# Linear attention and a top-1 mixture of experts on one core: routing arrays and k's maximum moved into PSUM, logits scaled on GpSimd, weight halves on VectorE, and the queues in another order

## The chip, the cores and the metric

The kernel runs on one NeuronCore of one Trainium2 chip. The metric is the device time of one execution in microseconds (us). Its five engines are written as in the profile: PE (TensorE, with PEld for its weight loads), DVE (VectorE), ACT (ScalarE), POOL (GpSimd) and SP (SyncE, which here only issues transfers). Each engine takes its instructions strictly in the order in which the program lists them, so an instruction that waits holds up everything behind it on its engine.

## What is computed

Inputs are `q`, `k`, `v` of shape 8 x 8 x 576 x 64 (batch, heads, sequence, head size), a gate matrix of 512 x 8, and two weight matrices for each of eight experts. The reference, cut to what matters:

```python
q_s = exp(q - max(q, axis=-1));  q_s /= sum(q_s, axis=-1)      # softmax over the 64 of a head
k_s = exp(k - max(k, axis=2));   k_s /= sum(k_s, axis=2)       # softmax over the 576 of the sequence
x   = einsum('bhsd,bhde->bhse', q_s, einsum('bhsd,bhse->bhde', k_s, v))   # then 4608 tokens x 512
logits = x @ w_gate                                            # 4608 x 8
expert = argmax(logits);  gate = softmax(logits)[expert]
out = gate * (relu(x @ w1[expert]) @ w2[expert])
```

## The kernel before, in words

The program has three stages.

*Attention.* The eight batches are taken one by one. For each batch SP loads k, v and q. DVE takes k's maximum (`k_max`, lines 135 to 141, step `ka`) over the nine rows that a partition holds: a chain of four instructions that halve nine rows to one. PE turns the result (`kt`, line 147), DVE reduces it across what were partitions (`kr`, line 154), PE spreads it back (`kx`, line 161), ACT copies it to SBUF (`ky`, line 167). POOL subtracts it from k (`ks`, line 173, three pieces of three rows), ACT takes the exponential (`ke`, line 181), and PE accumulates k times v (`v`, lines 190 and 200) in two PSUM banks. DVE divides by the sums (`vd`, `vr`, `vm`, lines 206 to 213), PE and ACT turn the result and multiply it with the gate matrix (`vt`, `vc`, `vg`, `vh`, lines 219 to 234). For q, DVE takes row maxima (`qm`, line 240), POOL subtracts (`qc`, line 248), PE turns (`qt`, line 256), ACT takes the exponential (`qe`, line 261), PE forms the product (`x`, line 270), which also carries eight gate logits per head, and ACT copies it out of PSUM (`xo`, line 282). The denominators are then prepared and inverted (`xd`, `xr`, lines 286 and 290) and the logits multiplied with them (`xl`, line 296, on DVE).

*Routing.* Two batches make a pair, whose 1152 tokens lie as 9 tiles of 128. Twenty small steps (`route`, lines 315 to 415), each one `r` in the order, sum the logits, find the largest, make a one-hot array, count tokens before each one with matmuls (line 364 on), and compute the row and tile that each token will have among those of its expert. They are almost all on DVE and their arrays, of 9 or 72 numbers a partition, lie in SBUF. `store` writes the pair's tokens to DRAM.

*Experts.* Tokens are gathered in tiles of 128 by expert (`g`, line 519, an indirect transfer that POOL issues), split into high and low 16-bit parts (`ps`, `ph`, `pl`), multiplied with w1 (`f`, line 598), passed through relu (`fh`, `fl`), multiplied with w2 (`s`, line 632), scaled and scattered. The weights are split into high and low parts as well: for the first expert `sh` makes the high part on ACT and, for w1, `ss` scales on ACT (line 677) and `sp` subtracts on POOL (`split_low_pool`, line 682); for w2, `sl` does both in one DVE instruction (`split_low`, line 673). For the other experts `ah` and `aw` do so and write both halves to DRAM, and POOL issues the indirect loads of line 745 that bring them back. From tile 3 on, `run` repeats one fixed order for each tile; I call this the loop. The first expert is chosen before the last pair is routed (`fe`), so that three tiles (slots 0 to 2) can be gathered and multiplied early.

The order of attention and of the passage into the loop is not found by a scheduler when the kernel is built: two tables of steps, `ATTENTION` and `JOIN`, list it, and `emit` (line 975) issues each step's instructions on its engines in that order. `ka:3` is the maximum of batch 3, `ks:3:6:3` its rows 6 to 8, `r:2` the next two routing steps.

PSUM has eight banks. Before, three pools share them: `ps_t` with two one-bank buffers, which serve k's turned maximum, its spread copy, both accumulators of k times v and the routing counts in turn; `ps_q` with two one-bank buffers; and `ps_x` with two buffers of two banks for the products.

Of the kernel before, what the change touches and what calls it, by code (L numbers as in the profile page):

```python
# [59 lines left out]
class Attention:  # L60


    def __init__(self, nc, tc, ctx, kctx, q, k, v, w_gate, xsc, R, C):
# [71 lines left out]
    def k_max(self, L, g=None):  # L135
        V, gs, k, m = self.nc.vector, self.heads(g), L["kt"], self.tile(L, "m", self.k1, [P, HP, D])
        t = self.tile(L, "mw", self.k1, [P, HP, 4, D])
        V.tensor_tensor(t[:, gs], k[:, gs, 0:4, :], k[:, gs, 4:8, :], op=ALU.max)
        V.tensor_tensor(t[:, gs, 0:2], t[:, gs, 0:2], t[:, gs, 2:4], op=ALU.max)
        V.tensor_tensor(t[:, gs, 1], t[:, gs, 1], k[:, gs, 8, :], op=ALU.max)  # L140
        V.tensor_tensor(m[:, gs], t[:, gs, 0], t[:, gs, 1], op=ALU.max)
# [139 lines left out]
    def x_out(self, L, m):  # L281
        self.nc.scalar.copy(self.x_rows(L, m, 1)[:, 0, 0:XU].rearrange("p (a x) -> p a x", a=2), L["xp", m][:, :, 0:4 * KW])  # L282
# [9 lines left out]
    def x_logit(self, L, j, n):  # L292

        u = self.x_units(L, j, n)
        lg = u[:, :, :, D + 1:KW]
        self.nc.vector.tensor_tensor(lg, lg, u[:, :, :, D:D + 1].broadcast_to([P, n, H, NE]), op=ALU.mult)
# [18 lines left out]
    def route(self, L):  # L315
# [85 lines left out]
        def row_int():  # L401
            V.tensor_single_scalar(T["ri"][:, :], T["ri"][:, :], P - 1, op=ALU.bitwise_and)
# [8 lines left out]
        def tile_no():  # L411
            V.tensor_tensor(R["rt"][:, ts], T["rank"][:, :], T["rm"][:, :], op=ALU.subtract)
# [587 lines left out]
lk:0:0 xi:0 xi:1 xi:2 lk:0:1 lk:1 ka:0:0 ka:0:1 lq:0 kt:0 kr:0 kx:0 ky:0 ka:1 lv:0 ks:0:0:3 kt:1 kr:1 qm:0:0:4  # L1000
kx:1 ks:0:3:3 ke:0:0:3 qm:0:4:5 lk:2 ky:1 ks:0:6:3 ke:0:3:3 v:0:0:3 ks:1:0:3 ke:0:6:3 lq:1 v:0:3:3 ks:1:3:3
ke:1:0:3 v:0:6:3 ks:1:6:3 ke:1:3:3 vd:0 lv:1 vr:0 vm:0 qc:0:0:2 vt:0 ke:1:6:3 vc:0 qc:0:6:2 qm:1:0:4 qt:0:0 vg:0
qe:0:0 qc:0:4:2 qm:1:4:5 lk:3 vh:0 x:0:0 qc:0:2:2 qc:0:8:1 xo:0:0 qt:0:1 qc:1:0:2 v:1:0:3 qe:0:1 lq:2 qc:1:6:2
v:1:3:3 qc:1:4:2 v:1:6:3 qc:1:2:2 qc:1:8:1 lv:2 qt:0:2 vd:1 qt:0:3 ka:2 qe:0:2 x:0:1 qe:0:3 x:0:2 xo:0:1 vr:1
# [105 lines left out]
```

## Time and profile before

| what | value |
|---|---|
| median of three runs | 661.26 us (659.49 to 662.1) |
| profiled execution, its own time | 659.28 us |
| its span, first to last instruction | 657.6 us (1.7 us lie around it) |
| mean granted PE clock | 0.943 of full speed |
| PE, DVE, ACT, POOL busy | 84%, 55%, 40%, 51% of the span |
| first product of batch 0, last of batch 7 | start 28.6 us, end 167.8 us |
| first w1 matmul | 180.2 us |
| first w1 matmul of tile 3 (start of the loop) | 217.0 us |

How to read it: the averages over the span hide that the three stages have different limits. The loop and what ends it take 440.6 of the 657.6 us, and their code is the same in both kernels. A window is a stretch of the span, in us from its start; the profile gives busy time by engine for each. A wait is put down to the instruction that released it.

### The profile page before, as it was taken

The page shows a single profiled execution, that of the slowest core. Times are in us where ns is not written, and L with a number is a line of the kernel's source. Part 1 is how long each engine was busy: PE and PEld are TensorE (multiplying, and loading weights), DVE is VectorE, ACT ScalarE, POOL GpSimd, SP SyncE. Part 2 cuts the span into 40 slices and gives each one's busy share as a digit, 9 for nine tenths or more (in the row PEclk, how much of TensorE's full clock was granted, in tenths as well). Part 3 has the DMA queues.
Part 4 walks back from the last instruction along what each step waited for, and adds up shares of the span by engine and source line. Part 5 has one row for each costly group of instructions (what it writes and reads, how often), then busy time and mean ns, then how long its engine had stood idle before and what let it go on. Part 6 is the DMA issues. An engine that isn't in the chain of part 4 may idle for free.

```text
span 657.6 us, 18347 instructions
## 1 busy us (share of the span) xinstructions
...
## 2 busy tenths in 40 slices
...
GB/s 316 325 347 119 335 243 219 167 167 272 239 206 306 271 307 182 217 330 268 221 248 309 287 201 199 153 269 146 247 175 374 219 181 207 203 178 80 149 148 12
DMA packets 73526, 148.58 MB, mean 226 GB/s; under 512 B 32721, under 2 KB 32721, under 8 KB 69843
## 3 DMA queue, kind: packets, MB, share of 16 engines
...
HBM read 220.73 MB, written 50.42 MB: 412 GB/s over the span
## 4 chain that ended last, share of the span: by engine, by line
PE 19%; issue 19%; DMA 15%; POOL 14%; DVE 1%; POOLq 1%; ACT 1%; ACTq 0%
DMA w<-wh,widx 11%; PE ps_q L632 9%; POOL w L745 9%; PE ps_x L598 9%; DMA out_dram<-ysb,sm 4%; POOL xg L519 3%; POOL out_dram L640 2%; PE ps_t L580 1%; DMA wh<-qs 0%; POOLq L745 0%; ACT xn L561 0%; PE ps_t L869 0%; DVE qs L719 0%; DVE co L719 0%; DVE w L673 0%
## 5 line engine op out<-in xcount | busy, mean ns | idle before, releaser
L745 POOL DMA_INDIRECT w<-wh,widx x140 | 144.7, 1034 | 167.7 <-PE ps_q L632 121.3
L598 PEld LDWEIGHTS <-w 128*128 128x128 f16 x3744 | 213.0, 98 | 27.4 <-DMA w<-wh,widx 14.9
L632 PE MATMUL ps_q<-w,ht 128*128 128x512 f16 x936 | 215.2, 386 | 15.2 <-DMA w<-wh,widx 11.7
L598 PE MATMUL ps_x<-xt,w 128*128 128x128 f16 x3696 | 214.7, 220 | 15.7 <-DMA w<-wh,widx 10.3
L632 PEld LDWEIGHTS <-ht 128*128 128x128 f16 x936 | 90.9, 99 | 121.6 <-issue 20.8
L607 DVE SCALAR_TENSOR_TENSOR ht<-ps_x,ht 128x512 f16<-128x512 f32 x77 | 53.0, 691 | 135.1 <-ACT ht L603 135.1
L603 ACT ACTIVATE ht<-ps_x 128x512 f16<-128x512 f32 x77 | 45.6, 596 | 139.4 <-PE ps_x L598 112.6
L173 POOL TENSOR_TENSOR kt<-kt,ms 128x768 f32<-128x768 f32 x24 | 47.9, 2026 | 33.2 <-ACT ms L167 22.7
L640 POOL DMA_INDIRECT out_dram<-ysb,sm x39 | 43.9, 1126 | 39.5 <-ACT ysb L636 23.2
L636 ACT ACTIVATE ysb<-ps_q,sm 128x512 f32<-128x512 f32 x39 | 26.8, 687 | 71.1 <-issue 35.9
L519 POOL DMA_INDIRECT xg<-xsc,gidx x40 | 39.2, 980 | 23.1 <-DVE sl_rank L926 11.4
L561 ACT ACTIVATE xn<-xg,sm 128x512 f16<-128x512 f32 x39 | 28.3, 726 | 52.8 <-DVE sm L556 36.8
L200 PEld LDWEIGHTS ps_t<-vt,kt 64*64 64x64 f32 x1152 | 38.2, 154 | 14.3 <-issue 13.8
L566 DVE SCALAR_TENSOR_TENSOR xn<-xg,sm,xn 128x512 f16<-128x512 f32 x39 | 29.3, 751 | 31.4 <-ACT xn L561 31.3
L200 PE MATMUL ps_t<-vt,kt 64*64 64x128 f32 x1152 | 42.6, 305 | 2.7 <-issue 2.7
L248 POOL TENSOR_TENSOR qs<-qt,qm 128x512 f32<-128x512 f32 x32 | 37.1, 1187 | 9.9 <-PE ps_q L219 7.1
L553 DVE TENSOR_TENSOR xg<-xg 128x512 f32<-128x512 f32 x39 | 27.4, 702 | 10.6 <-DMA xg<-xsc,gidx 7.2
L719 DVE SCALAR_TENSOR_TENSOR qs<-kt,qs 128x1024 f16<-128x1024 f32 x20 | 24.0, 1222 | 12.8 <-ACT qs L712 12.8
L270 PE MATMUL ps_x<-kvb,qT 64*64 64x73 f32 x1152 | 29.2, 251 | 2.1 <-ACT xmain L282 1.1
L261 ACT ACTIVATE qT<-ps_q 128x512 f32<-128x512 f32 x36 | 20.8, 596 | 24.5 <-PE ps_q L256 17.4
L582 ACT COPY xt<-ps_t 128x1024 f16<-128x1024 f16 x29 | 29.2, 1007 | 0.6 <-PE ps_t L580 0.6
L270 PEld LDWEIGHTS ps_x<-kvb,qT 64*64 64x64 f32 x1152 | 24.9, 153 | 6.9 <-issue 4.0
(173 smaller groups left out, 536.2 us busy)
## 6 DMA issues: line engine op xcount, KB each, us to landing
...
```

What stands on the lines that cost most here:

```text
L173: (eng or self.nc.gpsimd).tensor_tensor(kt, kt, m.unsqueeze(2).broadcast_to([P, gs.stop - gs.start, n, D]), op=ALU.subtract)
L200: nc.tensor.matmul(L["kv", h][a * D:(a + 1) * D, c, :], kt[r, g, i, :], v, start=False, stop=(i == NR - 1 and c == 1))
L248: (eng or self.nc.gpsimd).tensor_tensor(qs.rearrange("p i g d -> p g i d"), L["qt"][:, :, j:j + n, :], m, op=ALU.subtract)
L270: self.nc.tensor.matmul(xp[i * D:(i + 1) * D, a, u * KW:(u + 1) * KW], L["qT", m][r, 2 * i + c, h * D:(h + 1) * D], kvb[i][r, c, h, :], st ...
L519: self.nc.gpsimd.indirect_dma_start(out=self.xg[j % self.NX][:, :], out_offset=None, in_=self.xsc[0:rows, :], in_offset=bass.IndirectOffse ...
L566: self.nc.vector.scalar_tensor_tensor(self.heads(xn[:, 1, :]), self.xv(j), self.sm[j % self.NX][:, 2:3], self.heads(xn[:, 0, :]), op0=ALU. ...
L598: self.nc.tensor.matmul(ps[:, s * P:(s + 1) * P], self.w1[c // 2][:, c % 2, lo, f], xt[:, a, :], start=(c == 0 and k == 0 and s == 0), sto ...
L603: self.nc.scalar.activation(self.ht[j % 2][:, hf, 0:4, :].rearrange("p s t -> p (s t)"), ps, AF.Relu)
L607: self.nc.vector.scalar_tensor_tensor(ht[:, hf, 4:8, :].rearrange("p s t -> p (s t)"), ps, 0.0, ht[:, hf, 0:4, :].rearrange("p s t -> p (s ...
L632: self.nc.tensor.matmul(yp[:, :], ht[:, hf, a, :], self.w2[hf][:, s // 2, lo, s % 2, :], start=(c == 0 and k == 0), stop=(c == 7 and k == 2))
L640: self.nc.gpsimd.indirect_dma_start(out=self.out[:, :], out_offset=bass.IndirectOffsetOnAxis(ap=self.sm[j % self.NX].bitcast(I32)[:, 4:5], ...
L745: self.nc.gpsimd.indirect_dma_start(out=t.rearrange(flat), out_offset=None, in_=self.halves[which - 1][h][0:rows].rearrange("r a b f -> r ...
```

## The change

1. **PSUM shared out anew.** The two `ps_x` buffers are no longer handed out in turn. One (`xp`) holds every product, so there is one product buffer instead of two. Of the other, one bank (`room`) holds routing arrays, and one (`mx`) holds k's turned maximum and its spread copy, which leave the `ps_t` pool.
2. **Routing arrays in `room`** for the first three pairs: all arrays but `mx`, `ex` and `km`, the counts among them. The last pair keeps them in SBUF. `tile_no` masks bits and copies where it subtracted.
3. **k's maximum in one instruction**: `k_max` becomes a single reduction over nine rows, read with a step of 64 numbers. (Two new functions, `k_pair` and `k_max_pair`, are in the file, but no step of the tables calls them.)
4. **Logits scaled on POOL** instead of DVE (`x_logit`).
5. **w1's low parts for the first expert on DVE**: the tables use `sl` where they used `ss` and `sp`.
6. **Both tables are new**: the same steps in another order.

The diff, cut to its core (of the tables, a line each of many):

```diff
-        self.idle = self.ps_x.tile([P, 2, 512], F32, name="ps_x")[:, 0, :]
+        self.xp = self.ps_x.tile([P, 2, 512], F32, name="ps_x")
+        both = self.ps_x.tile([P, 2, 512], F32, name="ps_x")
+        self.room, self.mx, self.idle = both[:, 0, :], both[:, 1, :], both[:, 1, 0:256]
...
     def k_max(self, L, g=None):
-        V, gs, k, m = self.nc.vector, self.heads(g), L["kt"], self.tile(L, "m", self.k1, [P, HP, D])
-        t = self.tile(L, "mw", self.k1, [P, HP, 4, D])
-        V.tensor_tensor(t[:, gs], k[:, gs, 0:4, :], k[:, gs, 4:8, :], op=ALU.max)
-        V.tensor_tensor(t[:, gs, 0:2], t[:, gs, 0:2], t[:, gs, 2:4], op=ALU.max)
-        V.tensor_tensor(t[:, gs, 1], t[:, gs, 1], k[:, gs, 8, :], op=ALU.max)
-        V.tensor_tensor(m[:, gs], t[:, gs, 0], t[:, gs, 1], op=ALU.max)
+        gs, m = self.heads(g), self.tile(L, "m", self.k2, [P, HP, D])
+        self.nc.vector.tensor_reduce(m[:, gs], L["kt"][:, gs].rearrange("p g i d -> p g d i"), axis=AX.X, op=ALU.max)
...
-        L["mt", g] = mt = self.ps_t.tile([P, len(gg), 2, D], F32, name="ps_t")
+        L["mt", g] = mt = self.mx[:, 0:len(gg) * P].rearrange("p (a h q) -> p a h q", a=len(gg), h=2)
...
-        L["mb", g] = mb = self.ps_t.tile([P, len(gg) * 2, D], F32, name="ps_t")
+        L["mb", g] = mb = self.mx[:, 256:256 + len(gg) * P].rearrange("p (g d) -> p g d", g=2 * len(gg))
...
-        L["xp", m] = xp = self.ps_x.tile([P, 2, 512], F32, name="ps_x")
+        xp = self.xp
...
-        self.nc.vector.tensor_tensor(lg, lg, u[:, :, :, D:D + 1].broadcast_to([P, n, H, NE]), op=ALU.mult)
+        self.nc.gpsimd.tensor_tensor(lg, lg, u[:, :, :, D:D + 1].broadcast_to([P, n, H, NE]), op=ALU.mult)
...
+        room, used = (self.room if bp + 1 < NBP else None), [0]
...
         def t(name, shape, dt=F32):
-            T[name] = self.p2.tile(shape, dt, name=name)
+            if room is None or name in ("mx", "ex", "km"):
+                T[name] = self.p2.tile(shape, dt, name=name)
+            else:
+                n = shape[1] * (shape[2] if len(shape) > 2 else 1)
+                a = room[:, used[0]:used[0] + n]
+                used[0] += n
+                a = a if dt == F32 else a.bitcast(dt)
+                T[name] = a if len(shape) == 2 else a.rearrange("p (a b) -> p a b", a=shape[1])
...
         def tile_no():
-            V.tensor_tensor(R["rt"][:, ts], T["rank"][:, :], T["rm"][:, :], op=ALU.subtract)
+            V.tensor_single_scalar(T["ri"][:, :], T["ri"][:, :], -P, op=ALU.bitwise_and)
+            V.tensor_copy(R["rt"][:, ts], T["ri"][:, :])
...
-xd:7:4:1 xr:7:2:2 ph:1 xr:7:4:1 al:8 xl:7:2:2 sh:2:0 xl:7:0:2 xl:7:4:1 ps:0 rq:7 sh:2:1 al:11 sh:2:2 r:1 ph:0
+f:1:0 rq:7 ah:8 r:1 al:9 f:1:1 r:3 f:1:2 r:1 sh:2:0 r:5 sl:2:2 r:1 ah:9 sl:2:0 ah:10 f:1:3 ah:11 r:2 f:0:0 r:6
```

The last two lines are the heart of the new `JOIN`: the early tiles' w1 matmuls (`f:1`, `f:0`) now stand ahead of and among the last pair's routing (`rq:7` and the `r` behind it). Before, the first `f` stood behind all of it.

The order of the instructions on an engine, at three places. On DVE, in the middle of attention, around the second half of the first pair's routing, before (`rk` and `cnt` are the counts and their running sum, `ri` and `rm` integer rank and row, `m` k's maximum, `mw` its intermediate):

```order
93 L386 TENSOR_TENSOR rk<-ps_t,cnt 128x72
94 L390 TENSOR_TENSOR rk<-rk,oh 128x72
95 L393 TENSOR_TENSOR cnt<-cnt,ps_t 128x8
96 L396 TENSOR_REDUCE rank<-rk 128x9
97 L399 CAST ri<-rank 128x9
98 L138 TENSOR_TENSOR mw<-kt_168 128x1024
99 L139 TENSOR_TENSOR mw<-mw 128x4x128
100 L140 TENSOR_TENSOR mw<-mw,kt_168 128x4x64
101 L141 TENSOR_TENSOR m<-mw 128x256
102 L402 TENSOR_SCALAR ri<-ri 128x9
103 L405 CAST rm<-ri 128x9
```

The same stretch now, with `ps_x` as the name of the bank `room` (and, in the row of `cm`, of `mx`):

```order
62 L139 TENSOR_REDUCE m<-kt_171 128x256
63 L403 TENSOR_TENSOR ps_x<-ps_x,cnt 128x72
64 L407 TENSOR_TENSOR ps_x<-ps_x,oh 128x72
65 L410 TENSOR_TENSOR cnt<-cnt,ps_x 128x8
66 L162 TENSOR_REDUCE cm<-ps_x 128x4
67 L413 TENSOR_REDUCE ps_x<-ps_x 128x9
68 L416 CAST ps_x<-ps_x 128x9
69 L419 TENSOR_SCALAR ps_x<-ps_x 128x9
70 L422 CAST ps_x<-ps_x 128x9
```

Four instructions of k's maximum have become one, the routing arrays are all in PSUM, and the reduction for the next turned maximum (`cm`) stands in the middle of the routing.

On ACT, at the end of the last batch, before (`w_0`, `w_1` are w1's high parts, `kvt` and `kvb` the last batch's k-times-v result on its way to the products):

```order
99 L669 ACTIVATE w_0_192<-kt_170 128x1024
100 L677 ACTIVATE kt_170<-kt_170 128x1024
101 L669 ACTIVATE w_0_192<-kt_170 128x1024
102 L677 ACTIVATE kt_170<-kt_170 128x1024
103 L261 ACTIVATE qT<-ps_q 128x512
104 L223 COPY kvt<-ps_q 64x512
105 L282 COPY xmain_176<-ps_x 128x584
106 L286 ACTIVATE xmain_176<-xmain_176 128x4x8
107 L669 ACTIVATE w_1_193<-kt_168 128x1024
108 L234 COPY kvb_142<-ps_q 128x4x8
```

And now:

```order
118 L269 ACTIVATE qT<-ps_q 128x512
119 L294 ACTIVATE xmain_177<-xmain_177 128x4x8
120 L231 COPY kvt<-ps_q 64x512
121 L687 ACTIVATE w_1_194<-kt_169 128x1024 x2
122 L242 COPY kvb_142<-ps_q 128x4x8
```

`kvt` is copied ahead of all weight work instead of behind four pieces of it; `kvb` stands behind two pieces instead of five.

On POOL, at the start of the passage, before (`xg` are the gathered tiles):

```order
74 L302 IOTA xmain_177 64x4 x2
75 L305 IOTA xtail_180 64x1
76 L682 TENSOR_TENSOR w_0_192<-kt_170,w_0_192 128x1024 x2
77 L519 DMA xg_195<-xsc,gidx 128x588
78 L519 DMA xg_194<-xsc,gidx 128x588
79 L519 DMA xg_196<-xsc,gidx 128x588
80 L682 TENSOR_TENSOR w_1_193<-kt_168,w_1_193 128x1024 x2
```

And now:

```order
93 L313 IOTA xtail_181 64x1
94 L304 TENSOR_TENSOR xmain_177<-xmain_177 128x4x8x8
95 L537 DMA xg_196<-xsc,gidx 128x588
96 L537 DMA xg_197<-xsc,gidx 128x588
97 L537 DMA xg_195<-xsc,gidx 128x588
98 L304 TENSOR_TENSOR xmain_178<-xmain_178 128x2x8x8
```

The weight subtractions are gone from POOL; a scaling of logits stands ahead of the gathers instead.

More of the change, by code (lines that the diff above doesn't have):

```diff
@@ L281, in x_out @@
     def x_out(self, L, m):
-        self.nc.scalar.copy(self.x_rows(L, m, 1)[:, 0, 0:XU].rearrange("p (a x) -> p a x", a=2), L["xp", m][:, :, 0:4 * KW])
+        self.nc.scalar.copy(self.x_rows(L, m, 1)[:, 0, 0:XU].rearrange("p (a x) -> p a x", a=2), self.xp[:, :, 0:4 * KW])
     def x_den(self, L, j, n):
@@ L360, in count @@
         def count():
-            pr = T["pr"] = self.ps_t.tile([P, GT + 1, NE], F32, name="ps_t")
+            pr = T["pr"] = self.ps_t.tile([P, GT + 1, NE], F32, name="ps_t") if room is None else t("pr", [P, GT + 1, NE])
             ohf = lambda a, b: R["oh"][:, bp * GT + a:bp * GT + b, :].rearrange("p t n -> p (t n)")
@@ L999 @@
 ATTENTION = """
[L1000 to L1004, printed above, removed]
@@ L1025 @@
[L1025 to L1029 removed]
+lk:0:0 xi:0 xi:1 xi:2 lk:0:1 lv:0 ka:0:0 lk:1 ka:0:1 lv:1 kt:0 kr:0 kx:0 ka:1 ky:0 lq:0 ks:0:0:3 ks:0:3:3
@@ L1030 @@
+ke:7:3:3 r:1 x:6:0 r:4 xo:6:0 r:1 ks:7:6:3 qe:6:3 ke:7:0:3 x:6:1 r:3 v:7:0:3 fe qe:7:0 xo:6:1 ke:7:6:3 x:6:2 r:2
+qt:7:1 r:2 xo:6:2 r:1 v:7:3:3 qe:7:1 r:1 v:7:6:3 fc:1:2 !early x:6:3 fc:1:3 qt:7:2 xo:6:3 vd:7 xi:7 vr:7 vm:7
+qe:7:2 fc:1:0 xd:6:0:4 vt:7 xr:6:0:4 !early_ids vc:7 xl:6:0:4 fc:1:1 sh:1:2 vg:7 !early_index sl:1:2 ge:1 qt:7:3
+sh:1:3
 """
 JOIN = """
-!order fc:2:0 vh:7 ss:1:2 ge:0 qt:7:4 x:7:0 sh:1:3 fc:2:1 xl:6:0:4 ge:2 x:7:1 qe:7:3 sp:1:2 xo:7:0 fc:2:2 qe:7:4
-x:7:2 xo:7:1 fc:2:3 xd:7:0:2 ps:1 x:7:3 xo:7:2 ss:1:3 al:10 x:7:4 xo:7:3 xr:7:0:2 sp:1:3 xo:7:4 al:9 xd:7:2:2
@@ L1035 @@
-xd:7:4:1 xr:7:2:2 ph:1 xr:7:4:1 al:8 xl:7:2:2 sh:2:0 xl:7:0:2 xl:7:4:1 ps:0 rq:7 sh:2:1 al:11 sh:2:2 r:1 ph:0
-r:1 sh:2:3 r:3 pl:1 ah:8 r:5 ah:9 pl:0 r:1 sl:2:0 ah:10 ah:11 sl:2:1 r:9 !start al:13 !spread_pair:0 al:12
-!spread_pair:1 f:0:0 !spread_pair:2 f:1:0 ah:12 !spread_pair:3 f:1:1 ah:13 f:0:1 ps:2 f:1:2 sl:2:2 ph:2 f:0:2
-pl:2 al:14 f:1:3 sl:2:3 f:0:3 al:15 fh:0:0 !ids:0 fh:0:1 fl:0:0 fh:1:0 fl:0:1 s:0:0 fh:1:1 fl:1:0 s:0:1 fl:1:1
-s:0:2 s:1:0 aw:13 !ids:1 aw:12 !ids:2 !ids:3 aw:11 s:1:1 s:1:2 !index s:1:3 !ranks g:3 s:0:3 f:2:0 g:4 !turns
```

72 lines of the change are left out of this document (43 added, 29 removed), and 2 rows, old and new, of the table STEPS.

## The prediction

> **What bounds the kernel now.** I read the windows first, cut where the stages end: 17 us is shortly before the first k times v, at 152.4 the last batch's k times v is complete, at 217 the loop starts. The columns are the window, its length, busy time of PE, PEld, DVE, ACT and POOL (with instructions), the granted PE clock, the DMA share and GB/s.
>
> ```profile
> 17.00:152.40 135.40, 105.26 (x2561) 89.17 (x2559) 107.25 (x190) 63.07 (x119) 87.28 (x77) 0.89 0.64 233
> 152.40:217.00 64.60, 42.70 (x677) 34.10 (x678) 47.25 (x118) 30.91 (x46) 20.15 (x15) 0.79 0.81 271
> 217.00:657.60 440.60, 403.90 (x4568) 292.36 (x4567) 196.65 (x362) 166.60 (x224) 220.97 (x212) 0.98 0.65 214
> ```
>
> The loop is PE's: 403.9 of 440.6 us, 92%. Attention is nobody's: PE 78%, DVE 79%, one feeding the other. In the passage, PE works 66% of the time and DVE 73%. DMA is below its own 0.81 in attention, so transfers are not the limit there.
>
> Then the waits, PE's in attention and, in the last three rows, in the passage (who waited for whom, us in total, times, longest):
>
> ```profile
> PE ps_t L147 <- DVE m L141: 11.3, 3, 5.0
> PE ps_t L190 <- DVE cm L154: 7.5, 1, 7.5
> PE ps_t L190 <- DVE kvb L213: 4.5, 2, 2.8
> PE ps_q L219 <- DVE kvb L213: 2.1, 2, 1.2
> ...
> PE ps_t L364 <- DVE oh L355: 8.0, 1, 8.0
> PE ps_q L231 <- ACT kvt L223: 5.3, 1, 5.3
> PE ps_x L598 <- DMA xt<-xn: 3.7, 1, 3.7
> ```
>
> PE's idle time in attention is 135.4 − 105.3 = 30.1 us, and the first four rows make 25.4 of it: PE waits for DVE. Why DVE is late stands in its groups up to 200 us (line, operation, count, busy us, mean ns):
>
> ```profile
> L240 DVE TENSOR_REDUCE qm<-qt 128x16 f32<-128x1024 f32 (+1 forms) x16 | 20.9, 1338 | 0.0
> L138 DVE TENSOR_TENSOR mw<-kt 128x1024 f32<-128x1024 f32 (+1 forms) x9 | 10.6, 1172 | 3.9 <-DMA kt<-in_k_dram 3.9
> L139 DVE TENSOR_TENSOR mw<-mw 128x512 f32<-128x512 f32 (+1 forms) x9 | 9.7, 1079 | 0.3
> L140 DVE TENSOR_TENSOR mw<-mw,kt 128x256 f32<-128x256 f32 (+1 forms) x9 | 9.5, 1058 | 0.3
> L141 DVE TENSOR_TENSOR m<-mw 128x256 f32<-128x256 f32 (+1 forms) x9 | 9.1, 1006 | 0.3
> L296 DVE TENSOR_TENSOR xmain<-xmain 128x256 f32<-128x256 f32 (+1 forms) x9 | 6.7, 748 | 0.1
> L673 DVE SCALAR_TENSOR_TENSOR w<-st,w 128x1024 f16<-128x1024 f32 x4 | 4.8, 1217 | 0.0
> L333 DVE TENSOR_REDUCE lg<-xmain 128x32 f32<-128x256 f32 x8 | 4.5, 600 | 0.0
> L412 DVE TENSOR_TENSOR rt<-rank,rm 128x9 f32<-128x9 f32 x4 | 4.0, 993 | 0.0
> L390 DVE TENSOR_TENSOR rk<-rk,oh 128x72 f32<-128x72 f32 x4 | 3.7, 919 | 0.1
> L399 DVE CAST ri<-rank 128x9 int32<-128x9 f32 x4 | 3.6, 889 | 0.1
> L154 DVE TENSOR_REDUCE cm<-ps_t 128x4 f32<-128x256 f32 x8 | 3.3, 417 | 0.9 <-PE ps_t L147 0.8
> L355 DVE TENSOR_TENSOR oh<-key,km 128x72 f16<-128x72 f32 x4 | 3.0, 742 | 0.0
> L402 DVE TENSOR_SCALAR ri<-ri 128x9 int32<-128x9 int32 x4 | 2.3, 583 | 0.1
> L333 DVE TENSOR_REDUCE lg<-xtail 128x8 f32<-128x64 f32 x4 | 1.0, 254 | 0.0
> L396 DVE TENSOR_REDUCE rank<-rk 128x9 f32<-128x72 f32 x4 | 0.9, 229 | 0.0
> L386 DVE TENSOR_TENSOR rk<-ps_t,cnt 128x72 f32<-128x72 f32 x4 | 0.9, 228 | 0.8 <-PE ps_t L368 0.8
> ```
>
> Nine numbers take 993 ns on line 412, while 72 numbers with an operand in PSUM take 228 on line 386. Lines 139 to 141 halve the elements and hardly the time. These instructions are not working but held: two operands in SBUF, or a copy within SBUF, while POOL is at work. Reductions and instructions with an operand in PSUM are not held.
>
> **Attention, part by part.** *Routing arrays in PSUM.* Lines 412, 390, 399, 355 and 402 take 16.6 us for 20 instructions; at the 0.23 of line 386 they would take 4.6. The last pair's arrays stay in SBUF, but POOL is idle then, so its share is small: I count 12 us off DVE. *Logits to POOL:* line 296 with 6.7 us, of which about 1.4 are the last batch's after 152.4: 5 off DVE here. POOL's nearest row is this one:
>
> ```profile
> L248 POOL TENSOR_TENSOR qtl<-qt,qm 128x256 f32<-128x256 f32 x8 | 6.1, 758 | 6.9 <-PE ps_q L256 4.9 <-DVE qm L240 1.9
> ```
>
> Seven such are 5 us more on POOL, 92 of 135: not the bound. *k's maximum in one instruction.* The chain costs 38.9 us for eight batches, 4.9 each. What replaces it reads 2304 numbers with a step of 64. Contiguous reductions give (1338 − 417)/(1152 − 256) = 1.03 ns a number (lines 240 and 154; 1152 is the mean of the two forms, 1024 and 1280), so 2.5 us; the strided reductions of line 333 give (600 − 254)/192 = 1.80 ns, so 139 + 2304 × 1.80 = 4.3 us. The strided row is the nearer one: I take 4.3, hardly less than 4.9, 3.5 us over six batches, with 14 as the other end. [...]
>
> So DVE falls from 107 to about 86.5 us, and PE with 105.3 is then alone at the top. *The bank of their own* for the turned maximum lets `kt` run while k times v still holds its two accumulators; the one wait of 7.5 us, in which PE stood before line 190 until DVE had read the old maximum, has lost its ground. At the loop's 92% the stage would take 105.3/0.92 = 114.5 us, 21 less; at its present 78% nothing less. I take the middle, **−11**: the 7.5 whole and 3.5 of the other 17.9, since what stays (4.3 us of maximum, then the turn) still stands before PE. Late next are POOL's subtractions.
>
> [...] A result written to PSUM by DVE stands nowhere in this trace.
>
> **The passage.** Rows of ACT, POOL and DVE (start, duration, what, and the idle time before):
>
> ```profile
> 154.18 1.06 ACT L669 ACTIVATE w<-kt 128x1024 f16<-128x1024 f32 x1 [5.12 <-DMA kt<-in_moe_w_dram]
> 161.27 0.17 ACT L234 COPY kvb<-ps_q 128x32 f32<-128x32 f32 x1
> ```
> ```profile
> 156.45 4.39 POOL L682 TENSOR_TENSOR w<-kt,w 128x1024 f16<-128x1024 f32 x2 [7.93 <-ACT kt L677]
> 161.01 1.13 POOL L519 DMA_INDIRECT xg<-xsc,gidx  x1 [0.17 <-DVE sl_lead L887]
> ```
> ```profile
> 160.46 0.36 DVE L290 RECIPROCAL xmain<-xmain 128x32 f32<-128x32 f32 x1 [5.90 <-ACT xmain L286]
> 166.93 0.69 DVE L553 TENSOR_TENSOR xg<-xg 128x512 f32<-128x512 f32 x1 [5.39 <-DMA xg<-xsc,gidx]
> ```
>
> The last batch's `kvb` is copied at 161.27, behind five pieces of weight work for which ACT had waited until 154.18. Now two pieces of 1.06 stand before it: 154.18 + 2.1 = 156.3, 5 us earlier. The gathers stand behind 4.39 us of POOL's subtraction; now nothing of it is there, and they come about as much earlier. Both idle times of DVE, 5.90 and 5.39, hang on these two. Against that, four low parts of w1 come to DVE, 4 × 1.22 = 4.9 us (line 673), in front of the last pair's logits. 11.3 − 4.9 gives **−6.4**. On PE, the early tiles' w1 matmuls now fill the 8.0 us in which it waited for the one-hot array; with 5.3 and 3.7 it has 17 us of waits there, so DVE sets this term, with 47.25 + 4.9 = 52 us of work in 58. Bounds: nothing, if the transfers of the w1 pieces come later than before, and 11 if DVE closes up.
>
> *One product buffer instead of two.* Each product must now wait until ACT has copied the one before:
>
> ```profile
> L282 ACT COPY xmain<-ps_x 128x584 f32<-128x584 f32 x32 | 20.0, 647 | 6.6 <-PE ps_x L270 6.4
> ```
>
> The tables put other PE work between two products almost everywhere but for the last batch, where five follow each other: 5 × 0.65 = 3.2 us, of which PE waited 0.5 before. I add **+2**, from 0 to 23 (36 times 0.65, all in the open).
>
> **The sum.** −11 − 6.4 + 2 = −15.4. The profiled execution took 659.3 us (span 657.6, 1.7 around it), so 643.9 us: I say 644. The median of the three runs lies 2.0 above that execution and the fastest 0.2; I leave that difference to the range. The loop's own 440.6 I leave as it is.
>
> **The rivals.** *The order fills PE as in the loop.* A takes all of its 21 and the passage 10, for PE's waits there are 17 us: 659.3 − 31 + 2 = 630. For it: four of PE's five large waits name one engine. Against: at the start, loads and POOL set the pace. 0.15.
>
> *The strided maximum is slower than its row.* A step of 64 numbers isn't line 333's 73. At twice the price, 8.6 us, six batches add 22 to DVE, which eats the 20.5 taken off. Attention then gains only the passage's part and some of the 7.5: 659.3 − 4.4 − 2 = 653. Line 333 is the only strided row, so I can't exclude it. 0.13.
>
> *The single product buffer turns the sign.* If products stand in the open in more than 27 of the 36 cases (17.4/0.65), the gains are gone; at all 36, 659.3 − 17.4 + 23.3 = 665. Against it: line 282's idle time of 6.6 us says that ACT mostly comes to it late, not PE. 0.09.
>
> *No gain arrives.* The first load of another expert's weights hangs on halves that DVE makes and SP writes; if those transfers end at the same time as before, the loop waits for what the passage saved: 657 to 661. DMA has 0.81 of the passage's 64.6 us, 52 us, so six less still leave it at 0.9. 0.07.
>
> **How the numbers follow.** The forecast has 0.56; its own range, from the bounds of its three terms without their corners, is 635 to 652. The range for 8 in 10 takes in the strided maximum and most of the fuller case, and ends where the product buffer turns the sign: 628 to 660. It leaves out that case (0.09) and the lower part of the fuller one. A measurement can tell some 0.5% from no change, 3.3 us: faster means below 658. Forecast, strided and fuller case make 0.84, less 0.01 for their upper end: 0.83. The same 0.08, slower 0.09.
>
> **What would show it.** Where PE stands today (the last batch's products, the first w1 matmul, tile 3's):
>
> ```profile
> 162.54 2.23 PE L270 MATMUL ps_x<-kvb,qT 64*64 64x73 f32 x64
> ...
> 180.24 12.31 PE L598 MATMUL ps_x<-xt,w 128*128 128x128 f16 x192 [3.74 <-DMA xt<-xn]
> ...
> 216.96 5.52 PE L598 MATMUL ps_x<-xt,w 128*128 128x128 f16 x96 [1.10 <-ACT xt L582]
> ```
>
> In the new profile: k's maximum near 4.3 us, not 2.5; routing instructions near 0.23 us, not 1; line 190's successor without a wait of 7.5; products of the last batch from 150 to 155 us instead of 162.5; the first w1 matmul near 165; tile 3's near 202 instead of 217, and from there the same 440 us. The prediction is wrong if DVE is as busy as before at the same place, if PE's waits name ACT's product copy, or if the loop takes longer than 444 us.

## The result and the profile after

| | before | after |
|---|---|---|
| median, us (4 runs each, same chip) | 660.38 (657.15 to 662.10) | 637.81 (636.50 to 640.49) |
| ratio, 95% interval | | 0.967 (0.962 to 0.972) |
| profiled execution, its span, us | 659.28, 657.6 | 640.49, 638.8 |

The changed kernel is faster by 3.3%, 22.6 us between the medians. The two profiled executions lie 18.8 us apart, since after's was the slowest of its four; the steps below are measured between these two. A few executions of these kernels are over 1.5% slower than the rest (one of three_undone took 3089 us) and are left out of every ratio in this document, but the trace of logits_vector is of such a one, with its stretch of low clock in the loop. Windows of after, cut at the same events as before's: 17 us, the last batch's k times v, tile 3's first w1 matmul, the end (window, length, busy time of PE, PEld, DVE, ACT, POOL, granted PE clock, DMA share, GB/s).

```profile
17.00:134.50 117.50, 98.52 (x2531) 83.05 (x2523) 80.41 (x167) 62.48 (x119) 81.81 (x86) 0.94 0.76 277
134.50:194.70 60.20, 43.31 (x678) 34.80 (x678) 44.81 (x114) 28.52 (x45) 16.96 (x16) 0.83 0.72 231
194.70:638.80 444.10, 404.75 (x4568) 294.04 (x4567) 201.10 (x367) 165.28 (x221) 221.35 (x211) 0.98 0.66 217
```

Attention takes 117.5 us in place of 135.4 (−17.9), the passage 60.2 in place of 64.6 (−4.4), the loop 444.1 in place of 440.6 (+3.5): together the 18.8. In attention PE's idle time falls from 30.1 to 19.0 us, and its busy time falls too, from 105.3 to 98.5, at a granted clock of 0.94 in place of 0.89. What PE waits for there ("issue" is a wait for which the profile names no releaser) (us in total, times, longest):

```profile
PE ps_t L208 <- issue: 5.1, 4, 2.6
PE ps_x L278 <- issue: 3.8, 4, 1.7
PE ps_q L239 <- ACT kvt L231: 2.2, 1, 2.2
PE ps_q L264 <- issue: 1.9, 1, 1.9
...
PE ps_x L155 <- DVE ps_x L403: 1.6, 1, 1.6
...
PE ps_x L155 <- DVE m L139: 1.0, 1, 1.0
```

The four rows that named DVE with 25.4 us are gone; 2.6 us of such waits are left. But the waits without a named releaser have grown, from 3.4 to 11.2 us in all. DVE's groups up to 200 us, those that answer to the ones shown of before (line, operation, count, busy us, mean ns, idle before):

```profile
L139 DVE TENSOR_REDUCE m<-kt 128x256 f32<-128x2304 f32 (+1 forms) x9 | 33.7, 3754 | 5.8 <-DMA kt<-in_k_dram 5.8
...
L350 DVE TENSOR_REDUCE ps_x<-xmain 128x32 f32<-128x256 f32 x6 | 3.7, 619 | 1.4 <-ACT ms L175 0.6 <-PE ps_x L169 0.5
...
L357 DVE TENSOR_TENSOR ps_x<-ps_x,mx 128x72 f32<-128x72 f32 x3 | 0.7, 241 | 0.1
L407 DVE TENSOR_TENSOR ps_x<-ps_x,oh 128x72 f32<-128x72 f32 x3 | 0.7, 241 | 0.6 <-PE ps_x L155 0.5
...
L372 DVE TENSOR_TENSOR oh<-ps_x,km 128x72 f16<-128x72 f32 x3 | 0.7, 232 | 0.1
...
L416 DVE CAST ps_x<-ps_x 128x9 int32<-128x9 f32 x3 | 0.5, 175 | 1.3 <-PE ps_x L169 1.2
```

The maximum costs 33.7 us in place of 38.9, and the routing instructions that had taken 0.7 to 1 us take 0.18 to 0.24. But POOL gains too: its two subtractions before (lines 173 and 248) and after (lines 181 and 256), each up to the end of attention.

```profile
L173 POOL TENSOR_TENSOR kt<-kt,ms 128x768 f32<-128x768 f32 x24 | 47.9, 2026 | 33.2 <-ACT ms L167 22.7 <-issue 10.5
L248 POOL TENSOR_TENSOR qs<-qt,qm 128x512 f32<-128x512 f32 x32 | 37.1, 1187 | 9.9 <-PE ps_q L219 7.1 <-PE ps_q L256 2.8
```
```profile
L181 POOL TENSOR_TENSOR kt<-kt,ms 128x768 f32<-128x768 f32 x24 | 43.3, 1822 | 12.7 <-ACT ms L175 12.6
L256 POOL TENSOR_TENSOR qs<-qt,qm 128x512 f32<-128x512 f32 x32 | 32.9, 1056 | 11.3 <-PE ps_q L264 8.6 <-DVE qm L248 2.5
```

The same 24 and 32 instructions take 8.8 us less (2026 ns each before and 1822 now, 1187 and 1056), though nothing of them was changed: it looks as if what holds DVE holds POOL as well, and the experiments test this.

PE's rows after attention (start, duration, what, idle time before): the last batch's products, the first w1 matmul, tile 3's and tile 4's.

```profile
139.54 1.25 PE L278 MATMUL ps_x<-kvb,qT 64*64 64x73 f32 x32
...
143.78 0.74 PE L278 MATMUL ps_x<-kvb,qT 64*64 64x73 f32 x32 [0.77 <-ACT xmain L290]
145.56 0.74 PE L278 MATMUL ps_x<-kvb,qT 64*64 64x73 f32 x32 [1.03 <-ACT xmain L290]
147.66 1.25 PE L278 MATMUL ps_x<-kvb,qT 64*64 64x73 f32 x32 [1.37 <-ACT xmain L290]
152.90 5.91 PE L616 MATMUL ps_x<-xt,w 128*128 128x128 f16 x72 [3.98 <-DMA xt<-xn]
...
194.66 5.52 PE L616 MATMUL ps_x<-xt,w 128*128 128x128 f16 x96 [1.10 <-ACT xt L600]
...
210.18 7.15 PE L616 MATMUL ps_x<-xt,w 128*128 128x128 f16 x96 [4.38 <-ACT xt L600]
```

The products start at 139.5 (162.5 before), the first w1 matmul at 152.9 (180.2), tile 3's at 194.7 (217.0). Tile 4's comes 15.5 us after tile 3's; in before the same step took 12.2. There 3.3 of the 3.5 us are given back: PE waits 4.38 us for the turned tile, with POOL standing in front of the next expert's weights:

```profile
199.70 1.42 POOL L763 DMA_INDIRECT w<-wh,widx  x1 [0.30 <-issue]
211.67 1.01 POOL L763 DMA_INDIRECT w<-wh,widx  x1 [10.55 <-DMA wh<-qs]
```

### The profile page after: what moved, and what is told of

Same layout as the page of the kernel before. It is cut to its first block, busy times and chain, and to the rows that moved or that the text cites. A ratio compares the mean times of both kernels' runs of the same rounds, so it can differ in the third digit from the quotient of the medians.

```text
span 638.8 us, 18361 instructions
## 1 busy us (share of the span) xinstructions
PE 551.1 (86%) x7814; PEld 415.0 (65%) x7814; DVE 336.9 (53%) x666; ACT 259.6 (41%) x387; POOL 329.1 (52%) x360
## 4 chain that ended last, share of the span: by engine, by line
PE 34%; DMA 20%; issue 19%; POOL 15%; DVE 7%; ACT 3%; SPq 1%; POOLq 1%; ACTq 0%; DVEq 0%
PE ps_x L616 11%; PE ps_q L650 10%; DMA w<-wh,widx 10%; POOL w L763 8%; PE ps_t L208 4%; DMA out_dram<-ysb,sm 3%; PE ps_x L278 3%; POOL xg L537 3%; DMA kt<-in_k_dram 3%; PE ps_q L264 2%; POOL out_dram L658 2%; DMA xg<-xsc,gidx 2%; DVE qs L737 1%; PE ps_t L598 1%; DMA wgb<-in_moe_w_gate_dram 1%
## 5 line engine op out<-in xcount | busy, mean ns | idle before, releaser
L616 PEld LDWEIGHTS <-w 128*128 128x128 f16 x3744 | 216.2, 99 | 27.3 <-issue 11.1
L616 PE MATMUL ps_x<-xt,w 128*128 128x128 f16 x3696 | 217.8, 221 | 16.8 <-DMA w<-wh,widx 6.3
L181 POOL TENSOR_TENSOR kt<-kt,ms 128x768 f32<-128x768 f32 x24 | 43.3, 1822 | 12.7 <-ACT ms L175 12.6
L208 PE MATMUL ps_t<-vt,kt 64*64 64x128 f32 x1152 | 40.6, 290 | 8.0 <-issue 5.1
L208 PEld LDWEIGHTS ps_t<-vt,kt 64*64 64x64 f32 x1152 | 35.5, 144 | 12.5 <-issue 8.4
L278 PE MATMUL ps_x<-kvb,qT 64*64 64x73 f32 x1152 | 32.1, 249 | 7.7 <-issue 3.8
L256 POOL TENSOR_TENSOR qs<-qt,qm 128x512 f32<-128x512 f32 x32 | 32.9, 1056 | 11.3 <-PE ps_q L264 8.6
L139 DVE TENSOR_REDUCE m<-kt 128x256 f32<-128x2304 f32 (+1 forms) x9 | 33.7, 3754 | 5.8 <-DMA kt<-in_k_dram 5.8
L278 PEld LDWEIGHTS ps_x<-kvb,qT 64*64 64x64 f32 x1152 | 26.7, 150 | 13.2 <-issue 6.8
L290 ACT COPY xmain<-ps_x 128x584 f32<-128x584 f32 x32 | 20.7, 647 | 29.3 <-PE ps_x L278 29.1
## 6 DMA issues: line engine op xcount, KB each, us to landing
qt<-in_q_dram SPq DMA_DIRECT2D x8, 1152.0 KB, 15.5
```

The lines of the kernel that those rows point to most:

```text
L139: self.nc.vector.tensor_reduce(m[:, gs], L["kt"][:, gs].rearrange("p g i d -> p g d i"), axis=AX.X, op=ALU.max)
L181: (eng or self.nc.gpsimd).tensor_tensor(kt, kt, m.unsqueeze(2).broadcast_to([P, gs.stop - gs.start, n, D]), op=ALU.subtract)
L208: nc.tensor.matmul(L["kv", h][a * D:(a + 1) * D, c, :], kt[r, g, i, :], v, start=False, stop=(i == NR - 1 and c == 1))
L256: (eng or self.nc.gpsimd).tensor_tensor(qs.rearrange("p i g d -> p g i d"), L["qt"][:, :, j:j + n, :], m, op=ALU.subtract)
L278: self.nc.tensor.matmul(xp[i * D:(i + 1) * D, a, u * KW:(u + 1) * KW], L["qT", m][r, 2 * i + c, h * D:(h + 1) * D], kvb[i][r, c, h, :], st ...
L616: self.nc.tensor.matmul(ps[:, s * P:(s + 1) * P], self.w1[c // 2][:, c % 2, lo, f], xt[:, a, :], start=(c == 0 and k == 0 and s == 0), sto ...
```

## The experiments

My theory A was that VectorE and GpSimd hold each other and that the three edits to VectorE's work carry the gain; the rival B was that the new order alone does. Since the chips differ (the kernel before took 660 us on the first, 679 to 684 on the others), times are compared as ratios to before on the same chip. Attention shows no such difference (it ends at 134.5 and 133.7 us in two traces of the changed kernel, on two chips), so its end (end of the last division of k times v) is compared in us. That column has one execution for each run, so that a difference of 1 or 2 us in it says little.

| run | ratio (95%) | end of attention, us |
|---|---|---|
| before | 1 | 152.4 |
| after | 0.967 (0.962 to 0.972) | 134.5 |
| after, again | 0.970 (0.966 to 0.974) | 133.7 |
| old_order | 0.981 (0.976 to 0.985), 40 tiles | 141.4 |
| old_order_fixed | 0.989 (0.984 to 0.994) | 144.8 |
| before_kmax | 0.989 (0.983 to 0.995) | 145.3 |
| kmax_four | 0.977 (0.973 to 0.981) | 138.3 |
| routing_sbuf | 0.974 (0.969 to 0.978) | 132.9 |
| logits_vector | 0.967 (0.962 to 0.973) | 132.2 |
| two_undone | 0.967 (0.962 to 0.971) | 133.1 |
| three_undone | 0.985 (0.980 to 0.990) | 144.1 |
| more_reduce | 0.969 (0.963 to 0.974) | 135.0 |
| late_scale | 0.971 (0.965 to 0.977) | 135.0 |
| early_halves | 0.969 (0.964 to 0.973) | 134.2 |

### The new code in the old order

```
 ATTENTION = """
-lk:0:0 xi:0 xi:1 xi:2 lk:0:1 lv:0 ka:0:0 lk:1 ka:0:1 lv:1 ...
+lk:0:0 xi:0 xi:1 xi:2 lk:0:1 lk:1 ka:0:0 ka:0:1 lq:0 kt:0 ...
```

The tables of before stand in place of the new ones.

> The changed code (routing in PSUM, one-instruction maximum, logits on POOL, one product buffer, bank for the maximum's exchange), in the order of before, first expert's low parts back on POOL. Theory A, the freed VectorE carries the gain: PE's waits on VectorE in attention fall by 8 to 11 us without any new order, and the passage stays at its 64.6 us with the gathers behind POOL's split: 647 to 652 us. Theory B, the gain is the new order's: 658 us or more, with VectorE's busy time in attention down by some 20 us all the same and PE waiting there for something else.

A 40th tile ran here, for the reason that the next run's text gives, so its time is no answer. In the next run the copies are in place, here one of the 18:

```
-... x:3:0 qe:3:2 ... x:3:1 ... xo:3:1 vg:4 xo:3:0 ...
+... x:3:0 qe:3:2 ... xo:3:0 x:3:1 ... xo:3:1 vg:4 ...
```

> The changed code in the order of before, as in old_order, with 18 product copies moved ahead of the next products in the tables, as one product buffer asks (there two products were written before the first was copied out, tokens were routed wrongly and 40 tiles ran in place of 39). Theory A, the freed VectorE carries half of the gain without a new order: 640 to 648 us, first w1 matmul of the loop's weights 3 to 8 us ahead of before's 180.2. Theory B, the search brings all of it: 656 us or more.

Measured: 0.989, 7 of the 22 us, between the ranges of the two theories. DVE has as little to do in attention as in after (82.5 us there), and attention ends 7.7 us earlier than in before. PE's waits in attention say where the rest went:

```profile
PE ps_x L278 <- ACT xmain L290: 11.7, 15, 3.2
PE ps_x L169 <- DVE cm L162: 3.7, 2, 2.6
```

PE waits 11.7 us for the single product buffer in this order's attention, against 0.5 us there and 3.2 in the last batch in the new one. So one thing that the new order does is to pay for the bank.

### One edit alone: k's maximum in the kernel before

```
 def k_max(self, L, g=None):
-    V.tensor_tensor(t[:, gs], k[:, gs, 0:4, :], k[:, gs, 4:8, :], op=ALU.max)
-    V.tensor_tensor(t[:, gs, 0:2], t[:, gs, 0:2], t[:, gs, 2:4], op=ALU.max)
-    V.tensor_tensor(t[:, gs, 1], t[:, gs, 1], k[:, gs, 8, :], op=ALU.max)
-    V.tensor_tensor(m[:, gs], t[:, gs, 0], t[:, gs, 1], op=ALU.max)
+    self.nc.vector.tensor_reduce(m[:, gs], L["kt"][:, gs].rearrange("p g i d -> p g d i"), axis=AX.X, op=ALU.max)
```

> The kernel before with one edit: k's maximum as one reduction. In the changed kernel the four-instruction form cost 42.4 us of VectorE in place of 33.7 and 11 us of POOL, and 8.6 us of the end. Theory A1, VectorE and POOL free each other in any order: VectorE's time for it 38.9 -> 34, POOL's centring of k down from 2.03 us each by a tenth, 653 to 657 us. Theory A2, only an order that starts POOL early pays for the four instructions: POOL and VectorE shorter by the same, and 658 to 661 us, since the 7.5 us wait for the shared banks stays.

Measured: 0.989, 7 us, and attention ends 7.1 us earlier: by itself as much as all code edits together in the old order. A1 holds, at the favourable end of its range (0.989 of 660 is 653). POOL's groups up to 140 us:

```profile
L169 POOL TENSOR_TENSOR kt<-kt,ms 128x768 f32<-128x768 f32 x24 | 44.1, 1870 | 33.6 <-ACT ms L163 22.2 <-issue 11.3
L244 POOL TENSOR_TENSOR qs<-qt,qm 128x512 f32<-128x512 f32 x32 | 34.0, 1093 | 14.0 <-PE ps_q L252 13.9
```

POOL has 6.9 us less on these two (78.1 in place of 85.0). PE's accumulators still wait 3.6 us for the shared bank here, until DVE has read the maximum; in old_order_fixed, with a bank of its own for it, no such wait is left.

### Each edit undone in the new kernel

```
-        if room is None or name in ("mx", "ex", "km"):      # routing_sbuf
+        if room is None or name != "pr":
```
```
-        self.nc.gpsimd.tensor_tensor(lg, lg, ...)            # logits_vector
+        self.nc.vector.tensor_tensor(lg, lg, ...)
```

kmax_four puts the four lines of before_kmax's diff back; three_undone has all three edits undone, two_undone the first two.

> The changed kernel with the routing's small arrays back in SBUF; only the counts that PE writes stay in the bank. Theory A, VectorE and POOL hold each other: the 57 routing instructions of the first three pairs go from about 0.23 to 0.4 to 0.9 us when they meet POOL, VectorE in attention gains about 12 us of busy time, POOL's centring gets longer with it (mean of the keys' from 1.82 towards 2.03 us), and a third to a half of that reaches the end: 641 to 645 us. Theory B, the order brings it and VectorE has room left in it: 637 to 639 us.

> The changed kernel with the logits' scale on VectorE. In before it took 5.2 us there in six instructions of 0.87, 0.66 each on POOL now. Theory A: VectorE in attention +5 us, POOL -4.8; POOL is as busy there as VectorE (81.8 and 80.4 of 117.5 us), so no engine gains: 637 to 641 us. Theory B, POOL is the one that has room: 641 to 644 us.

> The changed kernel with k's maximum as four VectorE instructions through a one-buffered array. Theory A: VectorE's time for it goes from 33.7 to 38.9 us (+5.2), POOL is held by the first of the four, and the maximum stands ahead of the chain maximum, transpose, column, row, copy, centring of its batch; some 1 to 3 us reach the end: 639 to 641 us. Theory B, only the order matters: 637 to 639 us.

> The changed kernel with three parts undone: routing's arrays in SBUF, four-instruction maximum, logits on VectorE. What is left is the new order, the bank for the maximum's exchange, one product buffer and the first expert's low parts on VectorE. Theory A: VectorE's busy time in attention goes back from 80 to about 100 us, and 6 to 12 of the 22 us come back: 645 to 650 us. Theory B: 637 to 641 us.

Measured: with routing's arrays in SBUF, DVE has 93.0 us of work in attention in place of 80.4, as expected, and attention still ends no later (132.9). The ratio 0.974 is where theory A put it (641 to 645 us) and its interval still overlaps after's; by itself this run leaves the question open. The logits on VectorE change nothing (0.967). The maximum in four instructions takes back 0.7 to 1% (0.977, its interval apart from the one that after had first, 0.967, and touching the second, 0.970), more than the 1 to 3 us expected of theory A though attention ends only 3.8 us later, and all three undone take back more than half (0.985). The rows of the four-instruction maximum, DVE's and POOL's up to the same times:

```profile
L140 DVE TENSOR_TENSOR mw<-kt 128x1024 f32<-128x1024 f32 (+1 forms) x9 | 13.0, 1448 | 5.7 <-DMA kt<-in_k_dram 5.7
L141 DVE TENSOR_TENSOR mw<-mw 128x512 f32<-128x512 f32 (+1 forms) x9 | 11.6, 1290 | 0.3
L142 DVE TENSOR_TENSOR mw<-mw,kt 128x256 f32<-128x256 f32 (+1 forms) x9 | 10.2, 1136 | 0.3
L143 DVE TENSOR_TENSOR m<-mw 128x256 f32<-128x256 f32 (+1 forms) x9 | 7.6, 839 | 0.3
```
```profile
L185 POOL TENSOR_TENSOR kt<-kt,ms 128x768 f32<-128x768 f32 x24 | 46.9, 1970 | 13.6 <-ACT ms L179 13.5
L260 POOL TENSOR_TENSOR qs<-qt,qm 128x512 f32<-128x512 f32 x32 | 39.0, 1244 | 9.3 <-PE ps_q L268 7.3 <-DVE qm L252 1.9
```

It costs 42.4 us here, 8.7 more than the single reduction (in before it was 38.9), and POOL 9.7 us more. Which of the two counts?

### The same time on VectorE, without holding POOL

```
+        self.nc.vector.tensor_reduce(m[:, gs], L["kt"][:, gs, 0:3].rearrange("p g i d -> p g d i"), axis=AX.X, op=ALU.max)
         self.nc.vector.tensor_reduce(m[:, gs], L["kt"][:, gs].rearrange("p g i d -> p g d i"), axis=AX.X, op=ALU.max)
```

> The changed kernel with a second reduction ahead of each of k's maxima, over three of the nine rows, its result overwritten: 768 numbers more at 1.8 ns, 1.4 us for a batch, some 11 us of VectorE more in all, more than the 8.7 us that the four-instruction form cost, at the same place, but in instructions that neither hold POOL nor are held by it. Theory P, the four-instruction form costs because POOL is held (its centring took 9.7 us more there): POOL stays at its 82 us, attention ends at 133 to 136 us, time within 2 us of the changed kernel's. Theory V, it costs by VectorE's own time ahead of the batch's chain: attention ends at 138 to 140 us as with the four instructions (138.3), 4 us or more over the changed kernel.

The added reductions and POOL's two groups in this kernel:

```profile
L139 DVE TENSOR_REDUCE m<-kt 128x256 f32<-128x768 f32 (+1 forms) x9 | 8.4, 930 | 4.0 <-DMA kt<-in_k_dram 4.0
```
```profile
L182 POOL TENSOR_TENSOR kt<-kt,ms 128x768 f32<-128x768 f32 x24 | 43.3, 1822 | 16.1 <-ACT ms L176 16.0
L257 POOL TENSOR_TENSOR qs<-qt,qm 128x512 f32<-128x512 f32 x32 | 32.8, 1051 | 8.2 <-PE ps_q L265 6.9 <-DVE qm L249 1.2
```

The additions came out at 8.4 us, not 11, but that is the 8.7 of the four-instruction form, at the same place. POOL is as in after to 0.1 us, attention ends at 135.0, and the ratio is 0.969. Theory P holds: at this filling the four instructions cost because they and POOL hold each other, not by VectorE's time.

### Routing and logits undone together

> The changed kernel with routing's arrays in SBUF and the logits on VectorE; the one-instruction maximum and the new order stay. Each of the two undone by itself left the end of attention where it was or 1.6 to 2.3 us earlier (134.5, 132.9, 132.2 us), the maximum undone by itself put it 3.8 us later, all three 9.6 us later. Theory A', VectorE is no bound of attention until some 100 of its 117 us are filled (80.4 + 12.6 + 4.8 = 98 here): attention ends at 133 to 136 us and the time is the changed kernel's within 2 us. Theory A as it was put before, each held instruction costs its share: attention ends at 138 to 141 us, 4 to 6 us over the changed kernel.

> The changed kernel as it is, beside the next two on the same chip: 0.967 of the time before, as first measured (0.962 to 0.972).

Measured: 0.967 beside 0.970 for the changed kernel on the same chip, attention ends at 133.1 and 133.7. Attention's windows in this kernel, and with all three undone:

```profile
17.00:133.10 116.10, 97.39 (x2539) 82.56 (x2531) 99.16 (x176) 62.62 (x120) 79.25 (x77) 0.94 0.76 277
```
```profile
17.00:144.10 127.10, 100.79 (x2519) 86.18 (x2511) 109.96 (x195) 63.14 (x120) 89.19 (x77) 0.91 0.70 252
```

DVE (third busy time) is filled to 85% in the first and 87% in the second, yet they lie 11 us apart; POOL (fifth) has 10 us less in the first, since the single reduction leaves it alone. The end of attention for the four combinations:

| | maximum in four | in one |
|---|---|---|
| routing in SBUF, logits on VectorE | 144.1 | 133.1 |
| routing in PSUM, logits on POOL | 138.3 | 134.5 |

The end and the time are where theory A' put them. The maximum is worth 11.0 us where the others are undone and 3.8 where they are not; the other two are worth 5.8 or nothing. They aren't terms of a sum. POOL's two groups of subtractions show where the holding comes from: 76.2 us in after, 77.6 with routing and logits undone, 85.9 with the maximum undone, 88.0 with all three. So nearly all of what POOL feels is the four-instruction maximum. Routing and logits cost DVE's time alone, and that reaches the end only on top of the four instructions (110.0 of 127.1 us filled). The figure of some 100 us at which theory A' lets VectorE become the bound isn't shown: the four-instruction maximum costs at 89.0 of 121.3 us already. The single most useful piece is the maximum, and routing's bank and the logits could go back without loss in this order.

### The loop's start

late_scale moves the scaled copy of a gathered tile behind the last pair's exponential, and two low halves behind the ranks:

```
-... xl:7:2:2 ph:2 f:1:0 rq:7 ah:8 r:1 al:9 f:1:1 r:3 f:1:2 ... r:5 sl:2:2 r:1 ah:9 sl:2:0 ...
+... xl:7:2:2 f:1:0 rq:7 r:1 f:1:1 r:3 ph:2 ah:8 al:9 f:1:2 ... r:5 r:1 ah:9 ... sl:2:2 sl:2:0 f:0:2 ...
```

> The changed kernel with a part of its order changed, behind attention: the scaled copy of the third gathered tile (ScalarE, which stood 5.27 us for a transposed tile's transfer) goes behind the last pair's exponential, and two low halves of VectorE (2.3 us) behind the last pair's ranks. If the last pair's chain is what the loop's start waits for: the index of tokens 4 to 6 us earlier than 181.3, 633 to 636 us. If the expert weights' halves are (POOL stood 10.6 us for them at the loop's start): 636 to 639 us, with the earlier gathers in longer idle time.

DVE's rows of the last pair's chain, in after and in late_scale:

```profile
159.53 0.23 DVE L369 TENSOR_REDUCE gate<-ex 128x9 f32<-128x72 f32 x1 [3.62 <-ACT ex L358]
...
181.33 0.20 DVE L939 CAST gidx<-ps_t 128x40 int32<-128x40 f32 x1 [2.57 <-PE ps_t L887]
```
```profile
155.45 0.22 DVE L369 TENSOR_REDUCE gate<-ex 128x9 f32<-128x72 f32 x1
...
160.21 0.23 DVE L403 TENSOR_TENSOR rk<-ps_t,cnt 128x72 f32<-128x72 f32 x1 [3.99 <-PE ps_t L385]
...
180.69 0.20 DVE L939 CAST gidx<-ps_t 128x40 int32<-128x40 f32 x1 [1.90 <-PE ps_t L887]
```

The wait of 3.62 us went, and 3.99 us on PE's count came in its place, which stands on PE behind the first 72 w1 matmuls (they ran from 152.8). The index is 0.6 us earlier and the time the same (0.971): a wait was moved along its chain.

early_halves takes two of the six low halves out of the block ahead of the loop:

```
-... !ids:3 f:2:2 !index ... aw:14 ah:15 aw:15 aw:11 aw:12 al:19 aw:10 aw:13 al:18
+... !ids:3 aw:10 aw:11 f:2:2 !index ... aw:14 ah:15 aw:15 aw:12 al:19 aw:13 al:18
```

> The changed kernel with two of the next expert's low halves (the second quarter of w1) taken out of the block of six in front of the loop and put where VectorE waits 2.57 us for the index matmuls and the DMA engines stand idle. If the loop's start is where 3.5 us were given back: POOL's wait of 10.55 us for the halves falls below 5, tile 4's first w1 matmul (210.2) comes 2 to 4 us earlier, and the time is 2 to 4 us under the changed kernel's. If the weights' transfers bind the loop as a whole: the same start, and within 1 us of it at the end.

POOL's and PE's rows at the loop's start in this kernel:

```profile
201.45 2.00 POOL L763 DMA_INDIRECT w<-wh,widx  x1 [0.31 <-issue]
203.76 1.01 POOL L763 DMA_INDIRECT w<-wh,widx  x1 [0.31 <-issue]
```
```profile
195.41 7.15 PE L616 MATMUL ps_x<-xt,w 128*128 128x128 f16 x96 [1.10 <-ACT xt L600]
210.38 5.53 PE L616 MATMUL ps_x<-xt,w 128*128 128x128 f16 x96 [2.19 <-DMA w<-wh,widx]
```

POOL's wait of 10.55 us is gone altogether, as expected, and so is PE's wait of 4.38 for the turned tile; but tile 4 still comes 15.0 us after tile 3, and not 2 to 4 us earlier. Two things fill the step now: 2.19 us behind the weights' own transfer, and tile 3's matmuls, which took 7.15 us in place of 5.52. The second is the granted clock: it is 0.76 over these matmuls (1.00 over tile 3's in after), as over tile 4's in after, which also took 7.15 (after, then early_halves; the clock is the first number behind the bracket):

```profile
210.18:217.33 7.15, 7.15 (x99) 0.76 0.74 248
```
```profile
195.41:202.56 7.15, 7.15 (x100) 0.76 0.96 348
```

So the same loss of 1.6 us lies behind tile 4's start in after and ahead of it here, and tile 5 is the fairer mark (before, after, early_halves):

```profile
242.81 5.53 PE L598 MATMUL ps_x<-xt,w 128*128 128x128 f16 x96 [2.51 <-DMA w<-wh,widx]
```
```profile
224.96 5.53 PE L616 MATMUL ps_x<-xt,w 128*128 128x128 f16 x96 [2.00 <-DMA w<-wh,widx]
```
```profile
223.37 5.53 PE L616 MATMUL ps_x<-xt,w 128*128 128x128 f16 x96 [1.84 <-DMA w<-wh,widx]
```

It comes 25.9 us after tile 3 in before, 30.3 in after (31.4 in the trace of after, again) and 28.0 here. So POOL's wait for the halves is a part of what the loop gives back, 2.3 of 4.4 us at this mark, and another 1.6 is the clock. The end can't tell: the ratio is 0.969 beside 0.970, and 2.3 us are 0.35%, less than half the width of either interval. The DMA share is 0.89 in after's first 37 us of the loop and 0.68 in before's; no run took transfers away, and what they cost there stays open.

The new order with the banks of before was not run; that its steps would wait for one another's banks without end is my reading of the tables, and isn't shown. No version ran faster than the changed kernel by more than the intervals; two_undone equals it with less code.

## Why the prediction was right, point by point

- **The sum.** 644 was forecast; the profiled execution took 640.5 and the median is 637.8. That it came so near is partly luck: attention gained 6.9 us more than its term, and the loop, put at no change, gave 3.5 back. The marks came earlier than named: the last batch's products at 139.5 (150 to 155), the first w1 matmul at 152.9 (165), tile 3's at 194.7 (202).
- **What bounds.** Right: PE's waits for DVE, 25.4 us, are the ones that went (2.6 left). In part others took their place: waits without a named releaser are 11.2 us in place of 3.4.
- **DVE's work in attention.** 107 to about 86.5 was forecast; 80.4 came. The maximum was forecast at 4.3 us and took 4.2 to 4.3 for a full batch; routing instructions near 0.23 took 0.18 to 0.24. The sizes were right for the rows listed; the rest is rows that the step didn't list (line 408 fell from 1690 to 1353 ns, line 358 from 596 to 175). **What failed is their weight**: the step counted 12 us off DVE for routing, 5 for the logits and 3.5 for the maximum, "hardly less than 4.9", as if time off DVE were the gain. The runs show the opposite order: routing and logits undone together cost nothing, the maximum alone brings 7 us in the old order. The step left out that the hold is mutual: on DVE, line 412 in before takes 1010 ns beside POOL's line 248 (at 99.7 us) and 161 with POOL idle (at 181.7), and POOL's two groups take 85.0 us in before and 76.2 in after. POOL's share of it was in no term, though POOL's subtractions were named as late next.
- **The strided reading.** As a price, "hardly less than 4.9" stands; as a measure of what the single instruction is worth to the kernel it was wrong, for the strided reductions with one operand left POOL alone: 8.4 us more of them in more_reduce, and POOL's two groups took 76.1 us beside 76.2 in after.
- **Arrays in PSUM.** That no row showed DVE writing to PSUM turned out not to matter: line 372, which reads PSUM and writes SBUF, takes 232 ns, and line 407, which writes PSUM too, 241, against 229 for the row from SBUF (line 396 before). That is 3 to 12 ns more; and by two_undone, where DVE had 99.2 us of work in attention in place of 80.4 and attention ended no later, a larger price would hardly have shown.
- **Attention, −11.** It came to −17.9. The idle time fell by 11.1, the size of the term but not by its parts: of the four rows 22.8 us went where the step counted 11, and the waits without a releaser ate a good part of it. The other 6.8 is PE's busy time, which the step held fixed at 105.3. Some 2.1 of it is work done before 17 us (4.49 in place of 2.39 us; the new order loads the first v right behind the first k); the rest, about 4.6, goes with the granted clock, 0.94 in place of 0.89. What sets the clock isn't shown: no run here varied it alone. By itself the clock doesn't place the end: attention ended at 134.5 at 0.94 (after), and at 133.7 and 135.0 at 0.97 (after again, more_reduce). Of the 17.9, the runs give 8.3 to what three_undone keeps (the order with its bank) and 9.6 to the three edits. What in the order brings the 8.3 was not taken apart.
- **The passage, −6.4 and +2 for the product buffer.** It came to −4.4 in sum, as forecast, but the sum is luckier than its parts. Right: the `kvb` copy ends 4.8 us after attention in place of 9.0, the gathers start 2.4 us after it in place of 8.6. The last batch's products wait 3.2 us for ACT, the number worked out for five copies in a row; less the 0.5 of before that is +2.7, which the text put down as +2. Wrong: DVE should have set the stage, with 52 us of work in 58, and it had 44.8 in 60.2. Its two idle times fell from 13.1 to 5.4 us, less than the 11.3 counted, and new ones came, 3.6 of them behind ACT's exponential.
- **The single product buffer elsewhere.** "The tables put other PE work between two products almost everywhere" was true of the new tables (0.5 us) and false of the old (11.7 us): the rival that turns the sign was near in the old order.
- **The loop, 440.6 unchanged.** It took 444.1, just over the 444 at which the text called itself wrong; 3.3 of the 3.5 us are lost between tile 3 and tile 4. This is the rival in which no gain arrives, at a fifth of its size. The wait that it named (for the halves) is part of it: without it, in early_halves, tile 5 came 2.3 us sooner behind tile 3, too little for the end to show.
- **The other rivals.** The strided maximum was not slower than its row (4.2 us for the 4.3 worked out). The fuller order is halfway true: attention took 117.5 where it gave 114.5, the passage gained 4 and not 10.
